# K and V of tile pairs by seven block products, earlier statistics, and one Q group moved among the output units

## The chip, the cores and the metric

The kernel runs on one core of a Trainium2 chip. The metric is the device time of one execution in microseconds. Before the change it is 757.27 us (median of three runs, 757.07 to 757.32). Engines are named as in the profile: PE is TensorE (matmuls, with PEld for its weight loads), DVE is VectorE, ACT is ScalarE, POOL is GpSimd, and SP is the engine that issues most of the DMAs. L428 is line 428 of the kernel before.

## The reference

Two blocks share a layer norm of x (2048 tokens, 1024 features): linear attention with 32 heads, and a SwiGLU feed-forward with 3584 hidden features. The output is x + s * silu(ffn). What the change touches is the projection of the normalized x to q, k and v, and the phi applied to q and k.

```python
def _layernorm(x, axis=-1, eps=1e-5):
    m = jnp.mean(x, axis=axis, keepdims=True)
    v = jnp.var(x, axis=axis, keepdims=True)
    return (x - m) / jnp.sqrt(v + eps)

def _A_ref(x, wqkv, wo):
    B, S, D = x.shape
    H = 32; Dh = D // H
    qkv = transpose((x @ wqkv).reshape(B, S, 3, H, Dh), 2, 0, 3, 1, 4)
    q, k, v = qkv[0], qkv[1], qkv[2]
    phi = lambda t: jnp.where(t > 0, t + 1, jnp.exp(t)) + 1e-6
    pq, pk = phi(q), phi(k)
    kv = jnp.einsum("bhsd,bhse->bhde", pk, v)
    z = jnp.einsum("bhsd->bhd", pk)
    num = jnp.einsum("bhqd,bhde->bhqe", pq, kv)
    den = jnp.einsum("bhqd,bhd->bhq", pq, z)[..., None] + 1e-6
    return transpose(num / den, 0, 2, 1, 3).reshape(B, S, D) @ wo

x = A_x
xn = _layernorm(x, axis=-1)
s = _A_ref(xn, A_wqkv, A_wo)
g = _silu((_silu(xn @ w_gate) * (xn @ w_up)) @ w_down)
return x + s * g
```

## The kernel before

**Stages.** The kernel is one long program of three stages. The front (L256 to L596) normalizes x, transposes it, and computes K, V and most of Q. The second stage (L598 to L724) finishes Q, computes the attention output tile by tile and multiplies it with wo. The third (from L728, about 500 us) is the feed-forward and the output. Tokens are cut into 16 tiles of 128, four blocks of four tiles (512 tokens), and two passes of two blocks (1024 tokens).

**Order.** In the front, `tc.manual_schedule` fixes the order of PE, DVE, ACT and POOL to the order in which the Python code emits instructions; SP's order is left to the scheduler. In the second stage SP's order is fixed too. Each engine works strictly through its own stream, so an instruction that waits holds up everything behind it on that engine. Work for DVE that has no place of its own stands in the deque `later`, and `fill(n)` emits the next n entries at fixed points.

**A tile in the front.** `emit_B(i, c)` is the c-th of four products of tile i with the K and V weights, 8 matmuls of 512 columns each (L428). The first two are K: ACT makes exp and relu of each (L186, L187), and after the second DVE makes phi from them (L190, L191). The last two are V, copied by ACT (L446). `emit_C(i)` adds the tile's 8 outer products of phi(k) and v (129 columns, L457) to the sums `kvz_ps`; it stands behind the first product of the next tile. For tiles 4 to 15 the loop at L568 emits the four products, two fillers behind each, and `emit_C` of the tile before.

**Statistics and transposes.** `emit_stats` (two instructions, L322) and `emit_aggr` (L335) give mean and variance of a tile; `emit_rstd` (L349) turns those of a group of tiles into 1/std with three DVE and twelve POOL instructions of a few columns; `emit_norm` (L371) applies them. Tiles 0 to 7 are transposed on PE (`emit_T`, the copies out of PSUM by DVE and then ACT). Blocks 2 and 3 (tiles 8 to 11 and 12 to 15) are written to DRAM and read back by a transposing DMA, both from SP (`emit_xT_block`, L415 and L416). In `later`, block 2's write is entry 18, behind the statistics of tiles 8 to 13.

**Q by block products.** `QGroup` computes 256 columns of q for one pass of 1024 tokens. The product is a 2 x 2 block product done with seven block products in place of eight (28 matmuls of 512 columns for 32). Part a: M3 into X, ACT copies X to u, M4 into Y, DVE adds Y to u. Part b: M1 into Z, DVE adds Z to u; M5 is added to X and M2 to Y, which then hold two of the four results, and ACT makes exp and relu of each. Part c: N7 is added to X and N6 to Y, DVE subtracts each from u, and ACT makes exp and relu of the two results. Part d is phi on DVE. The operands of the products are block sums made by DVE beforehand: `xsum_ops(p)` (five instructions of 2048 columns, L138) for x, `wsum_ops` (four, L152 to L155) for each group's weights. There are eight groups (pass 0 and 1, four each): six stand inside tiles 9 to 14, two, `qa` and `qb`, at the start of the second stage.

**PSUM.** All products of these stages draw from one pool of five buffers (`psB`); a buffer is free again behind its last reader.

**Second stage.** `emit_KVZ` masks the sums (DVE). `emit_ND(b, t)` is a tile's numerator and denominator (L632) with DVE's division behind it, and `emit_OT` writes the tile to DRAM (from ACT) and reads it back transposed (from SP, L656). An output unit `s_unit` is 8 matmuls with wo (L669), two for each tile; there are 32. The sets `nd_at` and `row_at` say before which unit an ND tile or a part d is emitted. Behind the last tile's `emit_OT` the first gate and up weights are loaded, and their block sums are made (`sum_w`) when four units are left.

**Memory that is used twice.** The eight tiles `xp`, each a pair of x tiles, lie in the pool `wgu` whose buffers later hold the q results `pqT`, and the normalized tiles wait for their transposition in `ws_all`, which later holds the block sums of weights.

Of the kernel before, what the change touches and what calls it, by code (L numbers as in the profile page):

```python
# [21 lines left out]
def kernel(  # L22
# [11 lines left out]
    nc = tc.nc  # L34
# [159 lines left out]
    wqp = p12.enter_context(tc.tile_pool(name="wqp", bufs=1))  # L194
    phiw = p12.enter_context(tc.tile_pool(name="phiw", bufs=5))
    qtmp = p12.enter_context(tc.tile_pool(name="qtmp", bufs=2))

    wq_sb = wqp.tile([P, DC, D], BF16, name="wq_sb")
    NM_Q = D // FW
    pqT_tiles = {}  # L200

    def exp_tile():
        return phiw.tile([P, SP_TOK], BF16, name="e_t", tag="e_t")

    class QGroup:


        def __init__(self, p, m):
            w = wq_sb[:, :, m * FW:(m + 1) * FW]
            self.lhs, self.rhs = block_operands(w, ws_all[:, m // 2, m % 2]), x_operands(p)  # L210
            self.out = wgu.tile([P, 2, SP_TOK], BF16, name="pqT", tag=("wg_sb" if m % 2 == 0 else "wu_sb"))
            pqT_tiles[(p, m)] = self.out
            self.row = {}
# [35 lines left out]
        def part_d(self, i):  # L249
            emit_phi(self.out[:, i, :], self.row[i][:])  # L250

    ET = mybir.EngineType
    FRONT_ORDER = {ET.PE, ET.DVE, ET.Activation, ET.Pool}
    kvz_ps = [psA.tile([P, GPT, NDW], FP32, name=f"kvz{j}", tag="A") for j in range(NJ)]
    with ExitStack() as p1:
# [4 lines left out]
        wkv_sb = wpool.tile([P, DC, 2 * D], BF16, name="wkv_sb")  # L260
        NV = 3
        v_bufs = [wpool.tile([P, G, NDW], BF16, name=f"v_sb{k}") for k in range(NV)]
# [85 lines left out]

        def emit_rstd(i):  # L349

            mv, rstd, tiles = grp_state[grp_of[i]]
            n = len(tiles)
            a = small.tile([P, TPB], FP32, name="lna", tag="lna")
            nc.vector.tensor_scalar(out=a[:, 0:n], in0=mv[:, 0:n, 1], scalar1=EPS_LN, scalar2=None, op0=ALU.add)
            yi = rstd[:, 0:n].bitcast(I32)
            nc.vector.tensor_single_scalar(out=yi, in_=a[:, 0:n].bitcast(I32), scalar=1, op=ALU.arith_shift_right)
            nc.vector.tensor_scalar(out=yi, in0=yi, scalar1=-1, scalar2=0x5f3759df, op0=ALU.mult, op1=ALU.add)
            y = rstd[:, 0:n]
            w = small.tile([P, TPB], FP32, name="lnw", tag="lnw")
            eng = nc.gpsimd  # L360
            for _ in range(NR_ITERS):
                eng.tensor_tensor(out=w[:, 0:n], in0=y, in1=y, op=ALU.mult)
                eng.tensor_tensor(out=w[:, 0:n], in0=w[:, 0:n], in1=a[:, 0:n], op=ALU.mult)
                eng.tensor_scalar(out=w[:, 0:n], in0=w[:, 0:n], scalar1=-0.5, scalar2=1.5,
                                  op0=ALU.mult, op1=ALU.add)
                eng.tensor_tensor(out=y, in0=y, in1=w[:, 0:n], op=ALU.mult)
# [15 lines left out]
        def xn_blk_slot(b):  # L382
            o = xn_base + (1 - b % 2) * TPB * D
            return ws_flat[:, o:o + TPB * D].rearrange("p (t d) -> p t d", t=TPB).bitcast(FP16)
# [35 lines left out]
        kv_tiles = {}  # L420

        def v_of(i):
            return v_bufs[i % NV]

# [24 lines left out]
        def emit_B(i, c):  # L449
            emit_B_mm(i, c)  # L450
            emit_B_out(i, c)

        def emit_C(i):
            pk_sb, v_sb = pk_tiles.pop(i), v_of(i)
            for g in range(G):
                j, gi = divmod(g, GPT)
                nc.tensor.matmul(kvz_ps[j][:, gi, 0:P + 1], lhsT=pk_sb[:, g * P:(g + 1) * P],  # L457
                                 rhs=v_sb[:, g, 0:P + 1],
                                 start=(i == 0 and gi == 0), stop=(i == NT - 1),
                                 skip_group_check=True)  # L460
# [10 lines left out]


        later = deque()
        for b in range(2, NB):
            for t in range(TPB):
                later.append(lambda i=b * TPB + t: emit_stats(i, parts=(0,)))
                later.append(lambda i=b * TPB + t: (emit_stats(i, parts=(1,)), emit_aggr(i)))
            later.append(lambda i=b * TPB: emit_rstd(i))
            if b > 2:
                for t in range(TPB):  # L480
                    later.append(lambda b=b, t=t: emit_norm(b * TPB + t, xn_blk_slot(b)[:, t, :]))
                later.append(lambda b=b: emit_xT_block(b))
            else:
                norm_b2 = [lambda b=b, t=t: emit_norm(b * TPB + t, xn_blk_slot(b)[:, t, :]) for t in range(TPB)]
                norm_b2.append(lambda b=b: emit_xT_block(b))

        pos = 2 * TPB + 1 + 4
        later = deque(list(later)[:pos] + norm_b2 + list(later)[pos:])
        later.extend(xsum_ops(0))
        for m in range(NM_Q):  # L490
            later.extend(wsum_ops(wq_sb[:, :, m * FW:(m + 1) * FW], ws_all[:, m // 2, m % 2]))
        later.extend(xsum_ops(1))

        def fill(n):
            for _ in range(min(n, len(later))):
                later.popleft()()

        with tc.manual_schedule(engines=FRONT_ORDER):
# [62 lines left out]
            emit_T(TPB + 1)  # L561
            emit_B_out(3, 2)
            emit_B(3, 3)
            fill(2)

            Q0 = 2 * TPB + 1
            early = deque([(0, m) for m in range(NM_Q)] + [(NPASS - 1, m) for m in range(NM_Q - 2)])
            for i in range(TPB, NT):  # L568
                grp = QGroup(*early.popleft()) if i >= Q0 and early else None
                nf = 1 if grp else 2  # L570
                emit_B(i, 0)
                fill(nf)
                emit_C(i - 1)
                if grp:
                    grp.part_a()
                emit_B(i, 1)
                fill(nf)
                if grp:
# [3 lines left out]
                emit_B(i, 2)  # L582
                fill(nf)
                if i == TPB:
# [4 lines left out]
                if grp:  # L589
                    grp.part_d(0)  # L590
                    grp.part_d(1)
                fill(nf)
            emit_C(NT - 1)
            assert not later and not early
        gate([x_loads[i] for i in range(first_wave, NT)], marks[("B", 1)], sync=True)
        gate(wq_loads, marks[("B", 3)], sync=True)  # L596

    with ExitStack() as p2:  # L598
# [90 lines left out]
        with tc.manual_schedule(engines=FRONT_ORDER | {ET.SP}):  # L689

            qa, qb = (QGroup(NPASS - 1, m) for m in (NM_Q - 2, NM_Q - 1))
            for c in range(NCC):
                nc.sync.dma_start(out=wo_sb[:, :, c * CW:(c + 1) * CW], in_=wo_v[:, :, c * CW:(c + 1) * CW])
            emit_KVZ()
            qa.part_a()
            qa.part_b()
# [10 lines left out]

            rows = deque((grp, i) for grp in (qa, qb) for i in range(2))
            nd_at = {1, 2, 4, 6, 8, 10, 11, 12, 14, 15, 16, 18, 19}
            row_at = {3, 5, 7, 9}  # L710
            assert len(nd_at) == len(nds) and len(row_at) == len(rows)
            u = 0
            while units:
                if u in nd_at:
                    nd_tile()
                if u in row_at:
                    grp, i = rows.popleft()
                    grp.part_d(i)
                if len(units) == 2 * NCC:
                    sum_w(0, 0)  # L720
                    sum_w(0, 1)
# [377 lines left out]
```

## Time and profile before

| What | Value |
|---|---|
| runs | 757.27 us median (757.07 to 757.32) |
| the profiled execution | 756.84 us, its span 755.1 us |
| granted TensorE clock | 1.000 throughout |
| front, second and third stage by PE | about 0 to 166, 166 to 242, 242 to 755 us |
| tile 8 begins | 70.0 us |
| last L457 of the front | 166.4 us |
| output units | 179.5 to 242 us |
| DVE busy, 60 to 80 us | 16.1 of 20 us |
| DVE and ACT busy, 77.4 to 165.9 us | 47.8 and 53.6 of 88.5 us |

The span runs from the first to the last instruction on the core; the execution's own time has 1.7 us more. Busy time of an engine counts each instruction's whole record. Matmuls overlap in these records, so how fast they follow each other is read from their starts and not from their lengths. In the lists of groups the columns are line, engine, operation, out<-in, shapes, count, then busy us and mean ns of one, then the idle time before and who ended it.

### The profile page before, as it was taken

What the parts mean: (1) busy time and instruction counts of PE and PEld (TensorE: products, weight loads), DVE (VectorE), ACT (ScalarE), POOL (GpSimd) and SP (SyncE); (2) the same over time, 40 slices, a digit from 0 to 9 for tenths busy, and PEclk for the clock granted to TensorE, in tenths of its full rate; (3) what the DMA queues carried; (4) which work ended last, traced back from release to release, by engine and by line L of the source; (5) the groups of instructions that cost most, each with busy time, mean ns of one, the idle gap of its engine ahead of it and who ended that gap; (6) DMA issues with size and microseconds to landing.
All of it is one profiled execution on the core that took longest, in us unless ns stands there. A gap on an engine that the chain in (4) does not pass through costs nothing.

```text
span 755.1 us, 9916 instructions
## 1 busy us (share of the span) xinstructions
PE 745.4 (99%) x3724; PEld 351.9 (47%) x3764; DVE 482.9 (64%) x897; ACT 276.3 (37%) x482; POOL 52.6 (7%) x112
## 2 busy tenths in 40 slices
PE   8999999999999999999999999999999999999997
PEld 3554444445554444444444444444444444444454
DVE  6686666348854677786787776876754754445453
ACT  4444556555223434333433434343343011111111
POOL 3311000000000000000000000000000222222220
PEclk9999999999999999999999999999999999999999
DMA  9606100017799534663355733544869845454300
GB/s 317 222 20 181 44 1 0 1 34 204 207 226 289 160 104 130 188 196 112 102 163 150 215 102 120 174 147 123 288 231 352 295 181 181 181 181 155 110 29 29
DMA packets 127663, 115.98 MB, mean 154 GB/s; under 512 B 29440, under 2 KB 108416, under 8 KB 126336
## 3 DMA queue, kind: packets, MB, share of 16 engines
q1 hardware_dynamic: 122720, 106.58, 45.8%
q10 hardware_dynamic: 4896, 8.78, 3.4%
q8 instruction: 29, 0.48, 0.3%
q14 instruction: 18, 0.15, 0.1%
HBM read 70.52 MB, written 38.54 MB: 144 GB/s over the span
## 4 chain that ended last, share of the span: by engine, by line
PE 95%; DVE 2%; DMA 1%; ACT 1%; issue 1%; DVEq 0%; ACTq 0%
PE X L131 29%; PE Y L131 28%; PE kv_ps L428 14%; PE Z L131 10%; PE s_ps L669 6%; PE qY L131 3%; PE qX L131 3%; PE kvz L457 1%; PE qZ L131 1%; PE nd_ps L632 1%; DVE stats L322 0%; DMA oT<-o_dram 0%; PE tr_ps L397 0%; DMA o_dram<-o_sb 0%; DMA xp<-in_A_x_dram 0%
## 5 line engine op out<-in xcount | busy, mean ns | idle before, releaser
L131 PEld LDWEIGHTS <-ws_all 128*128 128x128 bf16 x1420 | 137.8, 98 | 162.6 <-issue 0.2
L428 PE MATMUL kv_ps<-wkv_sb,xnT 128*128 128x512 bf16 x496 | 114.2, 379 | 1.2 <-DVE xnT L411 0.5
L762 DVE TENSOR_TENSOR q<-n,Y 128x512 f32<-128x512 f32 x63 | 43.4, 688 | 108.1 <-PE Y L131 104.9
L131 PEld LDWEIGHTS <-xs 128*128 128x128 bf16 x616 | 58.0, 98 | 63.1
L1032 POOL TENSOR_TENSOR o_out<-y,xres 128x512 bf16<-128x512 f32 x29 | 35.2, 1214 | 648.8 <-DVE y L1031 648.8
L428 PEld LDWEIGHTS <-xnT 128*128 128x128 f16 x512 | 49.2, 98 | 57.6 <-DVE xnT L411 0.7
L131 PE MATMUL Y<-xs,ws_all 128*128 128x512 f16 (+3 forms) x308 | 70.3, 360 | 0.0
L131 PE MATMUL X<-xnT,ws_all 128*128 128x512 f16 (+1 forms) x278 | 70.1, 379 | 0.2
L131 PE MATMUL Z<-xs,ws_all 128*128 128x512 f16 x224 | 57.5, 379 | 0.0
L131 PE MATMUL Y<-xnT,ws_all 128*128 128x512 f16 x224 | 57.5, 379 | 0.0
L131 PE MATMUL X<-xs,ws_all 128*128 128x512 f16 x224 | 57.5, 379 | 0.0
L886 ACT ACTIVATE g<-cg 128x512 bf16<-128x512 f32 x56 | 35.3, 631 | 54.1 <-DVE cg L777 54.1
L768 DVE TENSOR_TENSOR u<-Z,q 128x512 f32<-128x512 f32 x63 | 43.3, 687 | 16.0 <-PE Z L131 15.9
L886 ACT ACTIVATE g<-X 128x512 bf16<-128x512 f32 x28 | 16.7, 597 | 99.4 <-PE X L131 99.4
L758 ACT COPY n<-X 128x512 f32<-128x512 f32 x63 | 36.9, 586 | 27.1 <-PE X L131 26.7
L911 DVE TENSOR_TENSOR ho<-g,up 128x1024 bf16<-128x1024 bf16 x56 | 38.2, 686 | 0.5
L1031 DVE TENSOR_TENSOR y<-y,s_in 128x512 f32<-128x512 f32 x31 | 22.2, 717 | 21.8 <-ACT y L1025 15.8
L131 PEld LDWEIGHTS <-wu_sb 128*128 128x128 bf16 x224 | 21.9, 98 | 26.4
L131 PEld LDWEIGHTS <-wg_sb 128*128 128x128 bf16 x224 | 21.9, 98 | 26.4
L673 ACT CAST s_sb<-s_ps 128x512 bf16<-128x512 f32 x32 | 18.5, 586 | 42.1 <-PE s_ps L669 35.1
L1025 ACT ACTIVATE y<-X 128x512 f32<-128x512 f32 x8 | 4.8, 598 | 69.7 <-PE X L131 61.2
L186 ACT ACTIVATE e_t<-kv_ps 128x512 bf16<-128x512 f32 x32 | 19.2, 599 | 29.6 <-PE kv_ps L428 27.3
(140 smaller groups left out, 1044.2 us busy)
## 6 DMA issues: line engine op xcount, KB each, us to landing
h_dram<-ho SPq DMA_DIRECT2D x56, 256.0 KB, 2.5
wg_sb<-in_B_w_gate_dram SPq DMA_DIRECT2D x14, 512.0 KB, 4.0
wu_sb<-in_B_w_up_dram SPq DMA_DIRECT2D x14, 512.0 KB, 4.3
wdr<-in_B_w_down_dram SPq DMA_DIRECT2D x14, 512.0 KB, 4.2
ws_all<-h_dram SPq DMA_DIRECT2D x4, 1792.0 KB, 8.5
wds_dram<-wdsA SPq DMA_DIRECT2D x14, 384.0 KB, 2.6
hp_a<-h_dram SPq DMA_DIRECT2D x3, 1792.0 KB, 9.8
o_dram<-o_sb ACTq DMA_DIRECT2D x16, 256.0 KB, 3.1
```

The source lines that it names most:

```text
L131: marks["mm"] = nc.tensor.matmul(acc[:, 0:c1 - c0], lhsT=lhs(k), rhs=rhs(k)[:, c0:c1], start=(first and k == 0), stop=(k == n - 1), skip_g ...
L186: nc.scalar.activation(out=e, in_=t, func=ACT.Exp)
L428: mm = nc.tensor.matmul(kv_ps[:], lhsT=xn_tok_ap(i)[:, dc, :], rhs=wkv_sb[:, dc, c * CW:(c + 1) * CW], start=(dc == 0), stop=(dc == DC - 1))
L669: mm = nc.tensor.matmul(s_ps[:], lhsT=oT[:, c, ttok], rhs=wo_sb[:, c, cc * CW:(cc + 1) * CW], start=(c == 0), stop=(c == G - 1))
L673: nc.scalar.copy(out=s_sb[:, cc * CW:(cc + 1) * CW], in_=s_ps[:])
L758: nc.scalar.copy(out=n[:], in_=self.X[:])
L762: nc.vector.tensor_tensor(out=self.q[:], in0=n[:], in1=self.Y[:], op=ALU.add)
L768: nc.vector.tensor_tensor(out=self.u[:], in0=Z[:], in1=self.q[:], op=ALU.add)
L886: nc.scalar.activation(out=self.g[:, i, j * TB:(j + 1) * TB], in_=src, func=ACT.Silu)
L911: nc.vector.tensor_tensor(out=self.ho[:, i], in0=self.g[:, i], in1=self.up[:, i], op=ALU.mult)
L1031: nc.vector.tensor_tensor(out=t[:], in0=t[:], in1=self.s_in[:, i, cs], op=ALU.mult)
L1032: (nc.vector if last and (i, j) != (0, 0) else nc.gpsimd).tensor_tensor(out=self.o_out[:, i, cs], in0=t[:], in1=self.xres[:, i, cs], op=AL ...
```

## The change

The front's loop is taken apart. Tiles 4 to 8 and tile 12 are still computed one by one, in the order 4, 5, 6, 7, 8, 12. K and V of the pairs (10, 14) and (11, 15), and K of the pair (9, 13), are computed by a new class `KVGroup` with the same seven block products as `QGroup`; V of (9, 13) stays plain. The two tiles of a pair lie in blocks 2 and 3, so the block sums of x for pass 1 serve as left operands, and ten new DVE sums of the K and V weights (`kv_sum_ops`) as right ones. These sums are stored in two pqT tiles, in quarters of xnT that nothing reads any more, and in place in `wkv_sb`. The groups follow each other in a written sequence `seq`; part c and the phi (`post`) of a group are emitted behind part a of the next.

In `later`, statistics of all tiles 8 to 15 now come ahead of block 2's norms, the second `emit_rstd` runs all its twelve small instructions on DVE, and two empty entries are put in behind it. The write of block 2 is entry 25. The loop's fills are larger for tiles 4 to 7 (3, 2, 2, 2) and one `fill(2)` is added in front of the last product of tile 3.

Of the eight Q groups one stands in tile 12, four and the first part of a fifth (`qa`) in `seq`, `qa`'s rest and `qb` at the start of the second stage, and the eighth, `qc`, before output units 2, 3 and 4. `nd_at` and `row_at` are shifted to fit.

```diff
-    phiw = p12.enter_context(tc.tile_pool(name="phiw", bufs=5))
+    phiw = p12.enter_context(tc.tile_pool(name="phiw", bufs=4))
...
+    def alloc_pqT():
+
+        for p in range(NPASS):
+            for m in range(NM_Q):
+                pqT_tiles[(p, m)] = wgu.tile([P, 2, SP_TOK], BF16, name="pqT", tag=("wg_sb" if m % 2 == 0 else "wu_sb"))
...
-        NV = 3
+        NV = 4
...
-        def emit_rstd(i):
+        def emit_rstd(i, eng=nc.gpsimd):
...
-            eng = nc.gpsimd
...
-            o = xn_base + (1 - b % 2) * TPB * D
+            o = xn_base + b % 2 * TPB * D
...
+        def kv_sum_ops(which, places):
+            w = wkv_sb[:, :, which * D:(which + 1) * D]
+            w11, w12, w21, w22 = w[:, 0:HD, 0:CW], w[:, 0:HD, CW:D], w[:, HD:DC, 0:CW], w[:, HD:DC, CW:D]
+            s1, s5, s2 = places
+            kv_rhs[which] = {"M4": lambda k: w22[:, k, :], "M3": lambda k: w11[:, k, :], "M1": lambda k: s1[:, k, :],
+                             "M5": lambda k: s5[:, k, :], "M2": lambda k: s2[:, k, :],
+                             "N7": lambda k: w21[:, k, :], "N6": lambda k: w12[:, k, :]}
+            tt = nc.vector.tensor_tensor
+            return [lambda: tt(out=s1, in0=w11, in1=w22, op=ALU.add), lambda: tt(out=s5, in0=w11, in1=w21, op=ALU.add),
+                    lambda: tt(out=s2, in0=w12, in1=w22, op=ALU.add),
+                    lambda: tt(out=w21, in0=w22, in1=w21, op=ALU.subtract),
+                    lambda: tt(out=w12, in0=w11, in1=w12, op=ALU.subtract)]
...
+        class KVGroup:
+
+
+            def __init__(self, which, t):
+                self.which, self.rhs = which, kv_rhs[which]
+                xop = x_operands(NPASS - 1)
+                self.lhs = {n: (lambda k, f=f: f(k)[:, t * P:(t + 1) * P]) for n, f in xop.items()}
+                self.tiles = [(NB - 2 + j) * TPB + t for j in range(2)]
...
+            def direct(self, i, j, acc):
+                if self.which == 0:
+                    cs = slice(i * CW, (i + 1) * CW)
+                    emit_exp_relu(self.e[j][:, cs], self.pk[j][:, cs], acc[:])
+                else:
+                    nc.scalar.copy(out=self.v_out(i, j), in_=acc[:].rearrange("p (g c) -> p g c", c=P))
...
+            def part_c(self):
+                for acc, which, i in ((self.X, "N7", 0), (self.Y, "N6", 1)):
+                    self.mm(acc, which, False)
+                    if self.which == 0:
+                        cs = slice(i * CW, (i + 1) * CW)
+                        r = self.pk[i][:, cs]
+                        nc.vector.tensor_tensor(out=r, in0=self.u[:], in1=acc[:], op=ALU.subtract)
+                        emit_exp_relu(self.e[i][:, cs], r, r)
+                    else:
+                        nc.vector.tensor_tensor(out=self.v_out(i, i), in0=self.u[:].rearrange("p (g c) -> p g c", c=P),
+                                                in1=acc[:].rearrange("p (g c) -> p g c", c=P), op=ALU.subtract)
...
+        later.extend(stats_ops(NB - 2) + [lambda: emit_rstd((NB - 2) * TPB)] + stats_ops(NB - 1))
+        later.extend([lambda: emit_rstd((NB - 1) * TPB, nc.vector), None, None])
+        for ops in (norm_ops(NB - 2), norm_ops(NB - 1), xsum_ops(0), ws_ops(0)):
+            later.extend(ops)
+
+        def more_ops():
+
+            alloc_pqT()
+            k_ops = kv_sum_ops(0, (pq_place(NPASS - 1, NM_Q - 2), pq_place(NPASS - 1, NM_Q - 1), x_quarter(0, 0, 1)))
+            v_ops = kv_sum_ops(1, (x_quarter(0, 1, 0), x_quarter(1, 0, 1), x_quarter(1, 1, 0)))
+            for ops in (ws_ops(1), xsum_ops(NPASS - 1), k_ops, v_ops[:1], ws_ops(2), v_ops[1:], ws_ops(3)):
+                later.extend(ops)
...
+            rest = list(range(TPB, 2 * TPB)) + [b * TPB for b in range(2, NB)]
+            fills = {2 * TPB: (2, 2, 1, 1), rest[-1]: (2, 2, 1, 1)}
...
+            for i in rest:
+                nf = fills.get(i, (3, 2, 2, 2))
+                if i == 2 * TPB:
+                    more_ops()
+                grp = QGroup(0, 0) if i == rest[-1] else None
...
+            seq = [(lambda: Q(0, 1), 1, 1), (lambda: K(1), 0, 1), (VPlain, 2, 2), (lambda: Q(0, 2), 1, 1),
+                   (lambda: K(2), 1, 1), (lambda: V(2), 2, 2), (lambda: Q(0, 3), 0, 0), (lambda: K(3), 0, 0),
+                   (lambda: Q(NPASS - 1, 0), 0, 0), (lambda: V(3), 0, 0), (lambda: Q(NPASS - 1, 1), 0, 0)]
+            prev = None
+            for make, fa, fb in seq:
+                grp = make()
+                grp.part_a()
+                fill(fa)
+                if prev:
+                    prev.part_c()
+                    prev.post()
+                else:
+                    emit_C(before)
+                if make is not seq[-1][0]:
+                    grp.part_b()
+                    fill(fb)
+                while ready_C:
+                    emit_C(ready_C.popleft(), last=(not ready_C and make is seq[-1][0]))
+                prev = grp
+            qa = prev
...
-            qa, qb = (QGroup(NPASS - 1, m) for m in (NM_Q - 2, NM_Q - 1))
+            qb, qc = QGroup(NPASS - 1, NM_Q - 2), QGroup(NPASS - 1, NM_Q - 1)
...
-            qa.part_a()
...
-            nd_at = {1, 2, 4, 6, 8, 10, 11, 12, 14, 15, 16, 18, 19}
-            row_at = {3, 5, 7, 9}
+            nd_at = {1, 2, 4, 6, 8, 11, 12, 13, 15, 16, 17, 19, 20}
+            row_at = {2, 3, 5, 7, 9, 10}
+            q_at = {2: qc.part_a, 3: qc.part_b, 4: qc.part_c}
...
+                if u in q_at:
+                    q_at[u]()
```

`KVGroup`'s parts a and b are those of `QGroup`, with its own names for the PSUM tiles (kX, kY, kZ) and with `direct` for the two results that part b completes: for K exp and relu by ACT, for V one copy by ACT.

## The prediction

> **What bounds the kernel now.** I read the page first, then TensorE's waits, then the timelines of TensorE, VectorE and the SP queue over the stretch that the change rebuilds (39 to 190 us), then the rows by shape.
>
> ```profile
> span 755.1 us, 9916 instructions
> ...
> PE 745.4 (99%) x3724; PEld 351.9 (47%) x3764; DVE 482.9 (64%) x897; ACT 276.3 (37%) x482; POOL 52.6 (7%) x112
> ```
>
> ```profile
> PE w_ps L466 <- DVE warm L90: 1.2, 1, 1.2
> PE s_ps L669 <- DMA oT<-o_dram: 0.5, 2, 0.3
> PE kv_ps L428 <- DVE xnT L411: 0.5, 1, 0.5
> ```
>
> ```profile
> 49.86 0.39 PE L457 MATMUL kvz<-v_sb,pk_sb 128*128 128x129 bf16 x4 [0.20 <-ACT v_sb L446]
> ...
> 72.19 7.07 PE L428 MATMUL kv_ps<-wkv_sb,xnT 128*128 128x512 bf16 x32
> 79.09 0.62 PE L457 MATMUL kvz<-v_sb,pk_sb 128*128 128x129 bf16 x8
> ```
>
> A busy share of 99% proves little, since a matmul's record (379 ns) outlasts its slot. What shows the bound is starts: 32 matmuls take 72.19 to 79.09, 0.216 us each, and TensorE's whole list of waits is about 3 us. From 50 to 179 us I find no other hole (holes of exactly one slot every ten us or so are missing records). So TensorE's own instruction stream sets the end, a removed 512-column matmul is worth 0.216 us, and a new wait of TensorE is paid in full.
>
> **What is removed.** A K or V product of two tiles was 2 x 2 x 8 = 32 matmuls; by block products it is 7 x 4 = 28. Five groups use it (K of 9/13, 10/14, 11/15; V of the last two): 20 matmuls, 20 x 0.216 = 4.32 us. The 129-column matmuls (L457) and all eight Q groups stay; one Q group of 28 x 0.216 = 6.05 us moves from the front to the output units. So 4.32 is all that the removal can give.
>
> The stream of weight load and matmul has been priced lower elsewhere: the Trainium skill (TensorE: Matmul & The Clock Gate, section Back-to-back issue gap) says a 512-column matmul in such a stream costs about 131 ns, by which 20 would give 2.6 us and my sum would end 1.7 us higher. This trace disagrees with its 216 ns, and the measurement decides.
>
> **What is added, by engine.** Rows by shape (after the bar: busy us, mean ns of one, then idle time before):
>
> ```profile
> L138 DVE TENSOR_TENSOR xs<-xnT 128x2048 f16<-128x2048 f16 x10 | 11.8, 1218 | 0.0
> L191 DVE TENSOR_TENSOR pqT<-e_t,pqT 128x1024 bf16<-128x1024 bf16 x16 | 11.1, 692 | 2.3 <-ACT pqT L187 1.9
> L231 DVE TENSOR_TENSOR qu<-qu,qY 128x512 f32<-128x512 f32 x8 | 5.5, 687 | 10.2 <-PE qY L131 10.2
> L228 ACT COPY qu<-qX 128x512 f32<-128x512 f32 x8 | 4.7, 586 | 2.5 <-PE qX L131 2.3
> L186 ACT ACTIVATE e_t<-pqT 128x512 bf16<-128x512 bf16 x16 | 9.9, 621 | 9.6 <-DVE pqT L246 9.6
> ```
>
> VectorE: ten weight sums of 2048 elements at 1.22 = 12.2 us, and four combinations of 0.69 in each of five groups = 13.7 us. ScalarE: one copy of 0.59 a group, less two copies in each V group. From the start of tile 8 to the last L457 TensorE then has tile 8 (7.4), tile 12 with a Q group (13.4), nine groups of 28 matmuls, the plain V of 9/13 with 32, eight of the last Q group's first part (292 x 0.216 = 63.1) and seven L457 batches of 0.46: 87.1 us. VectorE has 72 us in it: phi of tiles 8 and 12 (2.2), K groups 3 x (4 x 0.69 + 2 x 1.11) = 14.9, V groups 5.5, Q groups 25.6, sums 24.1 (weights of Q 5.8, block sums of x 6.1, the ten new ones 12.2). It fits in total, but each engine works in order, so lateness in single steps counts. I walked the steps with these durations.
>
> At nothing I take three edits. Four exp tiles for five: never more than four are live, and the oldest is given back by phi a whole step (6 us) before its next writer; a phi that late would stop ScalarE. The pqT tiles handed out at tile 8 need the last norm of tile 15, done near 63 us, while their first writer comes near 86. The sums' places in xnT and pqT were last read at least 5 us before (V's second and third sum follow the plain V products by 3 us).
>
> *Tiles 4 to 7.* Statistics of all eight tiles now come first; the write of block 2 moves from place 18 of the filler list to 25. Up to it VectorE has, from 39.51 us: eight tiles' statistics at 1.43 = 11.44, the first rstd 0.47, two phi at 1.14, two transposed copies at 0.29, four norms 1.92, and the second rstd, now on VectorE: 3 + 12 dependent instructions of four columns. VectorE shows only the first three, 0.16 long and 0.205 apart; between 0.16 (no gap) and GpSimd's 0.28 pitch I take 0.2, so 2.9 (2.3 to 3.9). With 0.6 idle at phi of tile 5 this ends at 59.6 instead of 56.5. Two costs:
>
> ```profile
> 56.52 0.39 SPq L415 DMA_DIRECT2D xn_dram<-ws_all  x1
> 61.27 3.99 SPq L416 DMA_TRANSPOSE xnT<-xn_dram  x1
> 68.63 0.39 SPq L415 DMA_DIRECT2D xn_dram<-ws_all  x1
> 72.94 4.04 SPq L416 DMA_TRANSPOSE xnT<-xn_dram  x1
> ```
>
> Write to landing is 4.75 us, then a transpose of 6.05 (10.8). Block 2 lands at 59.6 + 10.8 = 70.4; tile 8 wants it at 70.0. And block 3 is wanted by tile 12, now directly behind tile 8, at 77.4, no longer at about 118. Its norms are done by 63.3, but on SP its write stands behind block 2's transpose, which waits for its own write until 64.4 and then holds SP for 4.0: issue at 68.4, landing at 78.8 to 78.9. TensorE waits until then: **+1.5** in all, the 0.4 of tile 8 and 0.2 more at L457 (its ScalarE copy stands behind the later transposed copy) included. Should SP send block 3's write first, it lands in time and delays block 2's transpose instead, at most by its own three microseconds of data: +0.4 to +3.0. No case lies below nothing, since an earlier landing frees nothing that TensorE waits for today. GpSimd loses its twelve instructions (63.36 to 66.65 today), for which VectorE stood 3.4 us.
>
> *Groups.* Per step ScalarE has 5.4 us (a copy and eight activations) against 6.05 of TensorE where a K or Q group follows a K or Q group, plus 1.5 in which it must wait for VectorE's two combinations. Two such steps in a row stay inside the slack that N7 and N6 leave (0.7 and 0.6 us); V groups give it back. Where VectorE puts sums ahead of a subtraction the chain slips: K(2) holds V's two in-place sums, V(2) the sums of the last Q weights. By my walk K(2)'s N7 and N6 wait 0.25, V(2)'s N7 0.7 (its M5 copy stands behind K(2)'s four activations), C(12) 0.1: **+1.05** (0 to 3).
>
> *Last group.* L457 of 11 and 15 follows V(3)'s last products with nothing between: 0.16 drain + 0.69 subtraction against 0.86 of N6, then again for N6: **+0.35** (0, if later products go ahead of it, to 1.1).
>
> *Output units.* The moved Q group stands before units 2, 3 and 4, exactly where TensorE waits today:
>
> ```profile
> 184.34 3.63 PE L669 MATMUL s_ps<-wo_sb,oT 128*128 128x512 bf16 x16 [0.19 <-DMA oT<-o_dram]
> 188.78 3.40 PE L669 MATMUL s_ps<-wo_sb,oT 128*128 128x512 bf16 x15 [0.34 <-DMA oT<-o_dram]
> ```
>
> With the 0.16 by which a record outlasts its slot, 0.35 and 0.50 go: **-0.85** (-0.85 to +0.5: VectorE has 12.5 us of work in these 14.4). The first unit's cover shrinks by nothing: from Q part b to it the order is unchanged; the KVZ masks (2.0 us of VectorE) lose the first part but fit under part b's 2.6. The loads of the first gate weights are triggered one unit later (1.7 us); today they land at 234.7 and 236.2 and TensorE reaches their product at 242.5, so that hides.
>
> **Sum.** -4.32 + 1.5 + 1.05 + 0.35 - 0.85 = -2.3: span 755.1 to 752.8. The profiled execution took 756.84, 1.7 beyond its span, the median of the runs is 757.27: 755.0.
>
> **Rivals.**
> *No new waits* (chance 0.20): blocks 2 and 3 land in time, or ScalarE and VectorE stay ahead; -4.3 - 0.85 plus at most 1.5: 752.1 to 753.6. For it: ScalarE is busy 53.6 of 88.5 us from 77.37 to 165.9 today. Against: VectorE was busy 7.24 of 7.37 us in tile 7 already, and the SP rows leave block 3 no room.
> *Transposes collide* (0.14): write of 3 and transpose of 2 share the DMA queues, which either fills alone (about 380 and 290 GB/s), and the twelve small instructions take GpSimd's pitch: +3 to +4 in place of 1.5, so 756.5 to 757.5, no change.
> *ScalarE becomes the bound of the groups* (0.18), the slower side: each of the seven steps behind a K or Q group takes 5.4 + 1.5 = 6.95 instead of 6.05, 7 x 0.9 = 6.3; -4.32 + 1.5 + 6.3 + 0.35 - 0.85 = +3.0: 760.2. It decides from the point where ScalarE ends the activation of Y more than 2.6 us after M2, when N6 must wait. Against: steps behind V need only 3.0 us of ScalarE. What would start it is a PSUM buffer handed out late, but today kv_ps starts at 129.29 while VectorE's subtraction from X still runs (128.62 to 129.31), so X's buffer is not the next one used.
> *The forecast* (0.48): 753.9 to 756.4 around 755.0.
>
> About 0.2%, 1.5 us, can be told from no change. Faster by that: most of the forecast (0.42) and the first rival, 0.62; within it 0.06 and 0.12 of the collision, 0.18; slower 0.20. The range leaves out the slow case and the lowest tip: 752.5 to 758.0.
>
> **What the profile would show.** 512-column block products on kX, kY, kZ: 140, and 160 fewer L428. First matmul of tile 12 waiting for the transpose, released near 79 us, the block 3 write near 68.4. VectorE within 3 us of its work in the group steps, waits of TensorE on ScalarE at N7 or N6 of V(2). The two waits for oT before units 2 and 4 gone. I am wrong if TensorE has many waits of about 0.9 us from 100 to 160, or none at tile 12.

## The result, and the profile after

| | before | after |
|---|---|---|
| runs, median | 757.26 us (22 runs, 756.41 to 758.39) | 759.57 us (22 runs, 756.99 to 762.48) |
| ratio of after to before | | 1.0031 (95% interval 1.0021 to 1.0041) |
| the profiled execution | 756.84 us, span 755.1 | 760.91 us, span 759.1 |
| mean granted clock of the profiled execution | 1.000 | 0.996 |

The change made the kernel 0.31% slower; forecast was 0.3% faster, and the time lies outside the range. The removed work is gone all the same (3704 records of matmuls in place of 3724). Three far slower executions, one of e3 (870 us), one of e7 (2816 us) and one of the kernel before beside e5 to e8 (2833 us), enter no median and no ratio below. The page of the kernel after, and TensorE's waits (cause, us in total, times, longest):

```profile
span 759.1 us, 9917 instructions
...
PE 743.6 (98%) x3704; PEld 350.8 (46%) x3744; DVE 507.5 (67%) x939; ACT 275.9 (36%) x483; POOL 50.1 (7%) x101
```

```profile
PE s_ps L822 <- DMA oT<-o_dram: 3.0, 1, 3.0
PE kv_ps L440 <- DMA xnT<-xn_dram: 2.8, 1, 2.8
...
PE kv_ps L440 <- DVE xnT L419: 0.5, 1, 0.5
PE kvz L469 <- ACT v_sb L458: 0.5, 1, 0.5
PE kX L131 <- ACT v_sb L531: 0.4, 1, 0.4
```

Before, the longest wait for a transfer was 0.3 us. Now there are two of 3 us: at the first product of tile 8 (L440) and before output unit 0 (L822). The timeline of TensorE around tile 8, and the windows before and behind it (length, then busy us and instructions of PE, PEld, DVE, ACT and POOL, granted clock, DMA share, GB/s):

```profile
65.33 5.34 PE L440 MATMUL kv_ps<-wkv_sb,xnT 128*128 128x512 bf16 x24
73.50 2.72 PE L440 MATMUL kv_ps<-wkv_sb,xnT 128*128 128x512 bf16 x7 [2.82 <-DMA xnT<-xn_dram]
76.44 1.07 PE L469 MATMUL kvz<-v_sb,pk_sb 128*128 128x129 bf16 x8 [0.22 <-issue]
77.30 6.91 PE L440 MATMUL kv_ps<-wkv_sb,xnT 128*128 128x512 bf16 x31
```

```profile
70.00:74.00 4.00, 1.18 (x7) 0.37 (x5) 2.92 (x7) 0.58 (x1) 0.00 (x0) 1.00 1.13 232
74.00:77.40 3.40, 3.18 (x15) 1.74 (x15) 0.00 (x0) 0.66 (x2) 0.00 (x0) 0.50 0.91 205
```

The third number from the end is the clock: 1.00 during the wait, then 0.50 for 3.4 us, though TensorE is working again. The eight L469 take 0.86 us from the first to the next product there, 0.46 elsewhere. So one wait costs twice: 2.99 us until the data come, then 3.41 x 0.5 = 1.7 us of work at half clock. A profile whose clock stayed at 1.000 there (e3, below) agrees: from tile 8's first product to the first one behind the wait of V(2) it takes 60.11 us, the kernel after 61.78.

The sum of the prediction beside what the starts in this trace give (us beyond the usual pitch of each product):

| Step | Forecast | Measured |
|---|---|---|
| 20 products removed | -4.32 | -4.32 |
| L457 of tile 4 (later transposed copy) | +0.2 | +0.30 |
| tile 8 waits for block 2 | +0.4 | +2.99 |
| half clock behind it | not in the sum | +1.7 |
| tile 12 waits for block 3 | about +1 | 0 |
| K(2), V(2), C(12) | +0.25, +0.7, +0.1 | +0.29, +0.53, 0 |
| last group | +0.35 | +0.08 |
| unit 0 waits for oT | 0 | +3.15 |
| waits before units 2 and 4 | -0.85 | -0.85 |
| span | -2.3 | +3.9 (755.1 to 759.1 is +4.0) |

Three rows make the error: tile 8, the clock and unit 0 are 7.4 us over the forecast, and the rows of tile 12 and the groups give back some 1.3. Over the runs of this kernel the clock shows again: of the 22 times, the 14 with a mean granted clock of 0.997 or less lie at 758.82 to 762.48, the 8 above that at 756.99 to 759.57. (Up to 0.002 of the mean is half clock behind the last matmul, which costs nothing. Of 76 runs of the kernel before, taken beside e1 to e10, one has 0.997 and none less.)

### The profile page after: what moved, and what is told of

Its sections match the earlier page's. It is cut to its first block, busy times and chain, and to the rows that moved or that the text cites. A ratio compares the mean times of both kernels' runs of the same rounds, so it can differ in the third digit from the quotient of the medians.

```text
span 759.1 us, 9917 instructions
## 1 busy us (share of the span) xinstructions
PE 743.6 (98%) x3704; PEld 350.8 (46%) x3744; DVE 507.5 (67%) x939; ACT 275.9 (36%) x483; POOL 50.1 (7%) x101
## 4 chain that ended last, share of the span: by engine, by line
PE 91%; DVE 4%; DMA 3%; ACT 1%; issue 1%; DVEq 0%; ACTq 0%
PE X L131 29%; PE Y L131 28%; PE Z L131 10%; PE s_ps L822 7%; PE kv_ps L440 6%; PE qY L131 2%; PE qX L131 2%; PE kY L131 1%; PE kX L131 1%; DMA xnT<-xn_dram 1%; PE nd_ps L785 1%; PE kvz L469 1%; DVE stats L331 1%; DMA o_dram<-o_sb 1%; PE qZ L131 1%
## 5 line engine op out<-in xcount | busy, mean ns | idle before, releaser
L131 PEld LDWEIGHTS <-xs 128*128 128x128 bf16 (+1 forms) x716 | 67.6, 98 | 75.3 <-issue 1.2
L440 PE MATMUL kv_ps<-wkv_sb,xnT 128*128 128x512 bf16 x342 | 79.8, 383 | 3.8 <-DMA xnT<-xn_dram 2.8
L440 PEld LDWEIGHTS <-xnT 128*128 128x128 f16 x352 | 33.9, 99 | 42.7 <-DMA xnT<-xn_dram 3.3
L822 PE MATMUL s_ps<-wo_sb,oT 128*128 128x512 bf16 x123 | 29.0, 379 | 3.2 <-DMA oT<-o_dram 3.0
```

What stands on the lines that cost most here:

```text
L131: marks["mm"] = nc.tensor.matmul(acc[:, 0:c1 - c0], lhsT=lhs(k), rhs=rhs(k)[:, c0:c1], start=(first and k == 0), stop=(k == n - 1), skip_g ...
L440: mm = nc.tensor.matmul(kv_ps[:], lhsT=xn_tok_ap(i)[:, dc, :], rhs=wkv_sb[:, dc, c * CW:(c + 1) * CW], start=(dc == 0), stop=(dc == DC - 1))
L822: mm = nc.tensor.matmul(s_ps[:], lhsT=oT[:, c, ttok], rhs=wo_sb[:, c, cc * CW:(cc + 1) * CW], start=(c == 0), stop=(c == G - 1))
```

## Experiments

All are edits of the kernel after. The ratio is to the kernel before on the same chip; for the kernel after itself it is 1.0031. The waits (us beyond pitch) and the span are those of the one profiled execution.

| Run | median | ratio (95%) | span, clock | tile 8 | tile 12 | units 0 to 2 |
|---|---|---|---|---|---|---|
| e1_order | 757.78 | 1.0007 (0.9998 to 1.0016) | 755.2, 0.999 | 0.20 | 1.31 | 2.33 |
| e2_rstd_pool | 756.14 | 0.9987 (0.9978 to 0.9995) | 755.8, 0.996 | 0 | 0.28 | 3.01 |
| e3_qc_early | 759.30 | 1.0018 (1.0007 to 1.0028) | 755.3, 1.000 | 2.70 | 0 | 1.31 |
| e4_busy | 757.62 | 0.9999 (0.9990 to 1.0007) | 755.6, 0.999 | filled | 0 | 1.36 |
| e5_pool_qc | 755.37 | 0.9974 (0.9965 to 0.9983) | 753.2, 1.000 | 0 | 0.19 | 1.31 |
| e6_wo_half | 759.64 | 1.0033 (1.0014 to 1.0052) | 757.4, 0.996 | 2.84 | 0 | 2.39 |
| e7_pool_half | 756.15 | 0.9985 (0.9974 to 0.9997) | 754.0, 0.999 | 0 | 0.53 | 2.20 |
| e8_plain | 759.67 | 1.0031 (1.0019 to 1.0043) | 757.9, 1.000 | 0 | 0.64 | 2.21 |
| e9_wo_split | 756.12 | 0.9980 (0.9971 to 0.9989) | 755.0, 0.999 | 0.09 | 1.37 | 2.12 |
| e10_wo_only | 759.46 | 1.0028 (1.0019 to 1.0038) | 758.3, 0.996 | 2.76 | 0 | 2.78 |
| e11_cover | 754.86 | 0.9963 (0.9951 to 0.9975) | 753.1, 1.000 | 0 | 1.05 | 0.62 |

**The order on SP (e1_order).** The issue records of SP in the kernel after: block 2's write 60.07, block 3's write 63.59, block 2's transpose 64.45 to 70.53, block 3's transpose 70.63. The scheduler, which chose SP's order, put block 3's write ahead of block 2's transpose; the prediction had it behind. The edit holds it behind:

```diff
-            nc.sync.dma_start(out=blk_rows_pt(xn_dram, b), in_=xn_blk_slot(b))
-            nc.sync.dma_start_transpose(out=xn_blk_ap(b), in_=blk_rows(xn_dram, b))
+            wr = nc.sync.dma_start(out=blk_rows_pt(xn_dram, b), in_=xn_blk_slot(b))
+            gate([wr], marks.get("xT"))
+            marks["xT"] = nc.sync.dma_start_transpose(out=xn_blk_ap(b), in_=blk_rows(xn_dram, b))
```

> The changed kernel with one scheduling edge: block 3's write is issued on SP behind block 2's transpose. Theory (the write overtook on SP and shares the DMA engines with the transpose, which then lands at 73.45 us): block 2 lands at 60.1 + 10.8 = 70.9 and tile 8 waits 0.5 us in place of 3.0; block 3 is issued near 68.5, lands near 79, and tile 12 now waits about 1.0. No wait is long, so the granted clock stays 1.000 and the 1.7 us at half clock go: span 759.1 - 2.5 - 1.7 + 1.0 = 755.9. Rival (VectorE's lateness alone makes block 2 late, the order on SP is nothing): the transpose still takes 9 us from issue to landing, tile 8 waits 3.0 and the time stays near 759.6.

The queue of SP in e1 (start, length, line, transfer):

```profile
60.00 0.39 SPq L423 DMA_DIRECT2D xn_dram<-ws_all  x1
64.38 4.13 SPq L425 DMA_TRANSPOSE xnT<-xn_dram  x1
68.61 0.53 SPq L423 DMA_DIRECT2D xn_dram<-ws_all  x1
73.26 3.99 SPq L425 DMA_TRANSPOSE xnT<-xn_dram  x1
```

and in the kernel after, where the trace joins the pairs:

```profile
60.07 3.91 SPq L423 DMA_DIRECT2D xn_dram<-ws_all  x2
64.45 10.66 SPq L424 DMA_TRANSPOSE xnT<-xn_dram  x2
```

The write begins at the same time in both. Alone, block 2's transpose holds SP 4.13 us and lands 6.21 us after its start (70.59); beside block 3's write it holds SP 6.08 us and lands after 9.00 (73.45). That is the 3 us of tile 8. With the edit tile 8 waits 0.20, tile 12 waits 1.31, which are the prediction's numbers for its own order (0.4 and about 1). No half clock follows, and the kernel is 0.24% faster than the kernel after. Four of its 12 runs still have a clock of 0.997; the wait before unit 0 is left in it.

**The twelve small instructions (e2_rstd_pool).**

```diff
-        later.extend([lambda: emit_rstd((NB - 1) * TPB, nc.vector), None, None])
+        later.extend([lambda: emit_rstd((NB - 1) * TPB), None, None])
```

> The changed kernel with the second 1/std back on GpSimd, one argument less. Theory (collision on the DMA engines, set off because block 2's norms come 2.4 us later on VectorE): block 2's write goes at 57.7, its transpose at 62.4, ahead of block 3's write (63.6 or later), so it lands at 68.5 and tile 8 waits for nothing; block 3 lands by 77, in time for tile 12; clock 1.000. 759.1 - 3.0 - 1.7 = 754.4 span. Rival (the same collision at another time): block 3's write still stands ahead of the transpose, tile 8 waits 1 us or more. Rival (1/std on GpSimd holds VectorE up as it did before): block 3's norms wait 3 us and tile 12 waits 2 to 3.

Block 2's write starts at 57.58 in place of 60.07, and the scheduler's order on SP is that of e1 (transpose at 63.30, second write at 67.43). Both blocks land in time but for 0.28 us at tile 12, and the median falls 0.44%. The edit changes two things at once, the 2.5 us and the order; e1 shows the order alone. The span is 755.8 us where 754.4 was expected, and the clock of 0.996 in this profile comes from elsewhere than tile 8: it was 0.5 from 172.79 to 176.20, around the end of the 3.01 us wait before unit 0 (which starts at 173.53).

**The clock by itself (e4_busy).** Twelve matmuls of zeros into an unused PSUM tile stand where TensorE waits; nothing arrives sooner.

```diff
+                    d_ps = psB.tile([P, TB], FP32, name="d_ps", tag="B")
+                    for _ in range(12):
+                        nc.tensor.matmul(d_ps[:], lhsT=warm[:, 0:P], rhs=warm[:], start=True, stop=True)
```

> The changed kernel with twelve matmuls of zeros put in front of tile 8, 2.6 us of TensorE work that is in nobody's way while it waits 3.0 us for block 2. Theory (the wait itself lets the granted clock fall to one half for 3.4 us, in some executions and to different parts, and that makes the times spread from 757.0 to 762.5): clock 1.000 in all runs, the wait of tile 8's first real matmul the same, 757.2 in nearly all runs. Rival (the spread has another source, the DMAs for one): the runs still reach from 757 to 762.

Its timeline at tile 8 and the same two windows:

```profile
70.85 2.75 PE L686 MATMUL d_ps<-warm 128*128 128x512 bf16 x11
73.44 1.89 PE L440 MATMUL kv_ps<-wkv_sb,xnT 128*128 128x512 bf16 x8
75.17 0.62 PE L469 MATMUL kvz<-v_sb,pk_sb 128*128 128x129 bf16 x8
```

```profile
70.00:74.00 4.00, 3.95 (x19) 1.82 (x19) 3.26 (x7) 0.59 (x1) 0.00 (x0) 1.00 1.09 239
74.00:77.40 3.40, 3.40 (x24) 1.77 (x22) 0.00 (x0) 1.08 (x2) 0.00 (x0) 1.00 1.09 226
```

Tile 8 begins as late as in the kernel after, at 73.44 for 73.50, but at full clock, and none of the 11 runs has a clock under 0.998; they lie at 756.52 to 758.28, so the rival, another source of the spread, is out. The median is 0.32%, some 2.4 us, under the kernel after for more work done. The profiled half-clock stretch is worth 1.7 of it; how the other 0.7 splits between it and unit 0's wait, here 1.36 us and not 3.15, the runs do not tell.

**The wait before unit 0.** The engine queues of the kernel after (SP, then ACT, then TensorE):

```profile
163.62 1.80 SPq L846 DMA_DIRECT2D wo_sb<-in_A_wo_dram  x2
174.56 16.44 SPq L809 DMA_TRANSPOSE oT<-o_dram  x5
```

```profile
168.37 0.35 ACTq L808 DMA_DIRECT2D o_dram<-o_sb  x1
```

```profile
174.13 1.02 PE L131 MATMUL qY<-xs,ws_all 128*128 128x512 f16 x4
178.14 1.90 PE L822 MATMUL s_ps<-wo_sb,oT 128*128 128x512 bf16 x7 [2.99 <-DMA oT<-o_dram]
```

wo's 2 MB are issued behind the last L469 of the front and land at 170.17 and 173.39. The first tile's write (o_dram), issued at 168.37, lands at 174.54, 6.17 us later, and its transpose at 178.10. From wo's issue to oT there are 14.5 us; TensorE has 11.4 us of work in them (to 174.99). Before the change the chain was 166.58 to 179.02, 12.4 us (wo landed at 172.01 and 175.28, the write at 175.64), and TensorE had 12.9 us of work, to 179.46, because `qa`'s part a (1.73 us) stood there too. This edit puts matmuls there again, the moved Q group before units 0 and 1:

```diff
-            rows = deque((grp, i) for grp in (qa, qb, qc) for i in range(2))
+            rows = deque((grp, i) for grp in (qb, qc) for i in range(2))
...
-            row_at = {2, 3, 5, 7, 9, 10}
-            q_at = {2: qc.part_a, 3: qc.part_b, 4: qc.part_c}
+            row_at = {5, 7, 9, 10}
+            q_at = {0: lambda: (qc.part_a(), qa.part_d(0), qa.part_d(1), qc.part_b()), 1: qc.part_c}
```

> The changed kernel with the moved Q group's parts a and b before output unit 0 and part c before unit 1 (the phi of the first group goes ahead of part b). Theory (unit 0 waits for a chain of DMAs that starts when wo's load is issued behind the last L469, with the first o write behind wo's 2 MB): the transposed o lands about 14.5 us after that issue whatever TensorE does, so 4.3 us more of matmuls cover it, the 3.15 us wait goes, and the waits before units 2 and 4 do not come back: -3.1. Rival (the division on VectorE is late): the wait stays at 2 us or more, now with VectorE named ahead of it. The tile 8 wait and the half clock stay in both, so the times spread as in the changed kernel, around 756.4.

The wait for oT is gone. In its place part b's second product waits 1.31 us for the ScalarE copy of X, which follows part a too closely. The tile 8 wait stays. The profiled execution, which has no half-clock stretch, took 757.10 us, but the median is 759.30 where 756.4 was expected: by the ratios 0.13% below the kernel after, and the two intervals overlap. Four of the 9 runs have a clock of 0.996 or 0.997. Together with e2's edit:

> The twelve small instructions are back on GpSimd (as in e2) and the last Q group's parts stand before units 0 and 1 (as in e3). Theory (the kernel loses time only by TensorE's two 3 us waits and by the half-clock stretches that such a wait can start; the two waits are independent): no wait at tile 8, as in e2; the wait before unit 0 falls from about 3 to about 1.3 us, as in e3, too short for a half-clock stretch, so the clock is 1.000 in most runs: 1.5 to 2.5 us below e2, 753.6 to 754.6. Rival (the spread of e3's runs has another cause than tile 8's wait, for example the Q group's own place): clock 0.996 to 0.998 in most runs as in e3, 755.5 to 757.5.

The ratio is 0.9974, and no clock of the 9 runs is under 0.998: what was left of e3's time was tile 8's. Beside e2 (0.9987) that is 1.0 us, where 1.5 to 2.5 were expected, and the intervals overlap.

Does the write wait for wo? The second half of wo (read first by unit 1) is issued behind the first transpose, on the kernel after (e6) and with e2's edit (e7):

```diff
-            for c in range(NCC):
+            def load_wo(c):
                 nc.sync.dma_start(out=wo_sb[:, :, c * CW:(c + 1) * CW], in_=wo_v[:, :, c * CW:(c + 1) * CW])
+            load_wo(0)
...
             emit_OT()
+            load_wo(1)
             qa.part_c()
```

> Only the order of SP is changed against the kernel after: the second half of wo (columns 512 to 1023, read first by unit 1) is issued behind the transpose of the first ND tile, no longer in front of it. Theory (the first ND tile's write, issued about 4.5 us behind the loads of wo, queues behind their 2 MB and takes 6 us where 2 would do): the write lands within 2.5 us of its issue, the transpose about 2.5 us later, and TensorE reaches unit 0 with a wait of at most 0.5 us; the tile 8 wait and its half-clock stretch stay: 2 to 3 us below the kernel after, 756.5 to 757.5. Rival (the write is slow by itself, or the transpose is): the wait before unit 0 stays at 1.3 to 3 us and unit 1 waits for the second half as well: 759.5 to 762.

> e6's order of wo together with e2's GpSimd instructions: neither of the two 3 us waits should be left. Theory: clock 1.000 in most runs, TensorE's waits only about 0.3 at tile 12, 0.3 in K(2), 0.5 in V(2): span 755.1 - 4.32 + 0.3 (C of tile 4) + 0.3 + 0.3 + 0.5 - 0.85 = 751.3, time 753.1 (752.5 to 753.8), about 0.5% below the kernel before. Rival (each wait removed comes back elsewhere, at tile 12 or before units 1 and 2): 755 to 756.5, no better than e2.

SP's queue and TensorE's first wait in e7:

```profile
159.11 0.39 SPq L846 DMA_DIRECT2D wo_sb<-in_A_wo_dram  x1
166.26 1.24 SPq L809 DMA_TRANSPOSE oT<-o_dram  x1
167.55 0.57 SPq L846 DMA_DIRECT2D wo_sb<-in_A_wo_dram  x1
174.76 2.59 SPq L809 DMA_TRANSPOSE oT<-o_dram  x2
```

```profile
PE s_ps L822 <- DMA wo_sb<-in_A_wo_dram: 1.6, 1, 1.6
```

The mechanism held and the remedy failed. The write took 2.76 us in e6 and 2.38 in e7, for 6.17, and e7's oT landed at 169.37, 3.5 us ahead of TensorE. But unit 0 then waited until wo's second half landed (174.43), and no time was won: the rival's times. Unit 0 does not read that half; both halves lie in one tile, and with a tile for each (below) the wait at unit 0 is gone.

So e9 gives each half a tile, issues the second behind two transposes, and exchanges units 1 and 2 so that it is read later; e10 is the same without e2's edit.

```diff
-        wo_sb = wop.tile([P, G, D], BF16, name="wo_sb")
+        wo_h = [wop.tile([P, G, CW], BF16, name=f"wo_sb{c}") for c in range(NCC)]
...
+        units[1], units[2] = units[2], units[1]
...
             qb.part_b()
             emit_OT()
+            load_wo(1)
             nd_tile()
```

> e2 with wo in two tiles of its own (columns 0 to 511 and 512 to 1023), the second one's load issued behind the transposes of the first two ND tiles, and output units 1 and 2 exchanged, so that the second half is read two units later. Theory (in e6 and e7 the write and transpose of the first ND tile were on time, landed at 169.4 in e7 against TensorE's 172.8, and unit 0 waited only for the other half of the one wo tile): unit 0 waits at most 0.3 us, units 1 to 3 at most 0.5 together, clock 1.000 in most runs: 2.5 to 3 us below the profile of e2, span 752.0 to 753.0, median 753.7 to 755.0. Rival (the 2 MB of wo, 1 MB of transposes and writes fill the queues anyway, and what is late only changes its name): waits of 1.5 us or more before units 1 to 3, median 755.3 to 756.5 as e5 and e7.

> The kernel after with e9's order of wo and units alone; the twelve small instructions stay on VectorE. Theory (the wait before unit 0 and the one at tile 8 are independent, and unit 0's costs about 2.7 us more than before the change): the tile 8 wait of 3 us and its half-clock stretch stay, unit 0's goes: 2 to 3 us below the kernel after, 756.5 to 757.6, no change against the kernel before; the difference to e9 is 2.5 to 3.5 us. Rival (the wait before unit 0 is a follow-up of the tile 8 stall): unit 0 waits as in e9, but e9 and this are within 1 us.

Unit 0 starts with no wait in e9, 172.07, but units 1 and 2 wait 1.07 (oT of the second tile, 175.28) and 1.05 (wo, 180.26). e10 has 1.27 and 1.51 there. The expected 2 to 3 us did not come; the lateness changed its name, as the rival said. What did hold is the difference of the two, 0.9980 to 1.0028, 3.6 us (3.3 by the medians) against 2.5 to 3.5 expected: tile 8's wait with its half clock, independent of unit 0. It agrees with e2 against after (0.44%, 3.3 us).

What helps is again matmuls that need neither transfer. e11 is e9 with the last Q group's parts one to two units earlier:

```diff
-            row_at = {2, 3, 5, 7, 9, 10}
-            q_at = {2: qc.part_a, 3: qc.part_b, 4: qc.part_c}
+            row_at = {1, 2, 5, 7, 9, 10}
+            q_at = {0: qc.part_a, 2: qc.part_b, 3: qc.part_c}
```

> e9 with the last Q group's part a before unit 0 (the cover of 1.73 us that the change took away there), part b before unit 2 and part c before unit 3; qa's two phi one unit earlier. Theory (units 1 and 2 of e9 waited 1.07 and 1.05 us only because the second ND tile's transpose and the second half of wo land at 175.3 and 180.3, and matmuls that need neither can stand there): unit 1 is reached 1.7 us later and unit 2 after part b's 2.6 us, so no wait over 0.3 us before units 0 to 3: 1.5 to 2 us below e9's span but for the transposes' own scatter, span 752.0 to 753.5, median 753.8 to 755.2. Rival (what lands late moves with TensorE, since the ND tiles' writes stand behind TensorE's own products): waits of 1 us or more stay before units 1 to 3, median 755.5 to 756.5.

```profile
PE kv_ps L440 <- DMA xnT<-xn_dram: 0.9, 1, 0.9
PE kv_ps L440 <- DVE xnT L419: 0.5, 1, 0.5
PE kvz L469 <- ACT v_sb L458: 0.5, 1, 0.5
PE kX L131 <- ACT v_sb L531: 0.4, 1, 0.4
```

These are TensorE's waits in e11 but for the one of 1.2 us at the very start, which the kernel before has too. No unit waits any more for oT or wo (0.62 us go in an L785 batch at 177.4). The median, 754.86 us, is 0.37% under the kernel before and 0.68% under the kernel after, and the six runs spread over 1.2 us.

**What the removal is worth (e8_plain).** e7 with the five K and V groups computed plainly: 20 matmuls more, no sums, no combinations.

```diff
+            class Plain:
...
+                def part_a(self):
+                    emit_B(self.tiles[0], self.which * NCC)
...
+                def part_b(self):
+                    for j, c in ((0, 1), (1, 0), (1, 1)):
+                        emit_B(self.tiles[j], self.which * NCC + c)
...
+            K, V = (lambda t: Plain(0, t)), (lambda t: Plain(1, t))
```

> e7 with the five K and V groups computed plainly again in the same sequence (32 matmuls instead of 28 each, no weight sums, no combinations on VectorE), everything else as in e7. Theory (a removed 512-column matmul is worth 0.216 us, and the groups' own waits cost 0.8): 20 x 0.216 = 4.3, less 0.8 of waits that go with the groups, so 3.5 us above e7 (3.0 to 4.2). Rival (VectorE's and ScalarE's added work in the groups gives most of the saving back): at most 2 us above e7.

e8's median is 3.5 us above e7's, and its waits at K(2), V(2) and the last group are gone. The rival's 2 us at most is out: VectorE's 26.7 us more work in e7 from 60 to 165 us (83.84 against 57.12) are nearly all hidden.

## Why the prediction was wrong

**Right.** The price of a removed product (0.216 us) and the count: putting the 20 products back costs e8 3.5 us, and 4.32 less the 0.9 us of the groups' own waits is 3.4. The groups: 0.82 us measured for 1.05, in two of the three places named (nothing at C(12)); V(2)'s wait ended with the ScalarE copy behind K(2)'s four activations, as walked. The twelve instructions: 0.20 us apart in the trace, and the write at 60.07 for 59.6. The waits before units 2 and 4 went. ScalarE did not become the bound: no row of waits from 100 to 160 us but those of K(2) and V(2), so the rival at 760.2 had the time and not the mechanism.

**The step that failed first** is "but on SP its write stands behind block 2's transpose". SP's order in the front is the scheduler's, as the text before the prediction says, and it chose otherwise. The fallback in the same paragraph, "+0.4 to +3.0", has the right mechanism, and the 2.99 is its upper end; the sum went by the other order, and the two orders' waits cannot be averaged. The rival on colliding transposes named the same mechanism; the front alone (0.30 + 2.99) came out in its +3 to +4, without GpSimd's pitch.

**The step that was missing** is the granted clock. The prediction read it as 1.000 throughout and took a wait as worth its own length ("a new wait of TensorE is paid in full"). In the profile the wait of tile 8 cost 1.7 us more, and 14 of the 22 runs have a clock of 0.997 or less; with matmuls in that wait (e4) none of 11 has.

**The step that failed last** is "The first unit's cover shrinks by nothing" (its cover is the work that TensorE has while the transfers for it are under way). The order from part b on is indeed the same, but the cover has to be counted from the event that starts the late chain, and that is wo's issue behind the last L469. Part a of `qa` stood behind that event and now stands in front of it; the work behind the event fell from 12.9 to 11.4 us. Against the old chain of 12.4 that would have left a wait of 1.0; the other 2.1 is the chain itself, 14.5 us: wo's second half lands 9.77 us after the issue of the first in place of 8.70, the write lands 1.15 us behind it in place of 0.36, though it now follows wo's issue by 4.75 us in place of 6.26, and the rest takes 0.2 us more. That size is not fixed: the same code showed 1.36 to 3.15 us in four profiles (after, e1, e2, e4).

With the three taken away the sum is the forecast: e11, which has the change's groups, SP's order as forecast and cover before the late units, spans 753.1 us, and 755.1 - 2.3 is 752.8. Its single terms agree less closely: with the twelve instructions on GpSimd tile 8 does not wait at all, and 0.62 us among the units stands in place of that 0.4.

What stays open: why the scheduler chose SP's two orders, why wo takes 8.38 us in one profile (e4) and 9.77 in another (after), with the chain before unit 0 as long behind it, and in how many runs of the kernel after the wait there starts a half-clock stretch too. It did in e2's profile and not in that of after.

## What to carry to other kernels

When work is moved, count the cover of the next late transfer from the event that releases the transfer's chain, not from the work in front of its reader, and ask for each queue whether its order is written down or chosen. Price a wait of TensorE of about 3 us at up to 1.7 us above its length, paid in some runs and not in others, and fill it with other matmuls first: moving products in front of a late reader gave more here (e11) than trying to make the transfer earlier (e6, e10). A transfer that looks like the cause may only be the last of several; e6, e9 and e10 each freed one and met the next.

## What the runs showed of the hardware

**Half clock after a wait.** Waits of TensorE of 2.76 (e10), 2.84 (e6), 2.99 (after) and 3.01 us (e2) were each followed by one stretch of 3.41 us at clock 0.5, which began between 0.7 us before and 0.5 us after TensorE went on. Waits of 2.70 (e3, tile 8) and 3.15 us (after, unit 0) were not, nor any of 2.4 us or less. The Trainium skill (TensorE: Matmul & The Clock Gate, section What's actually happening) has the array at half rate after at least one idle window of about 3.4 us, in windows that run freely. That the stretch lasts 3.41 us and comes in some runs only agrees with this; that a wait of 2.8 us is enough does not, by its letter, and the measurement decides.

The records of the clock show what decides in place of the wait's length. In the 13 profiles every stretch of one clock, up to the last change, is a whole number of windows of 3.413 us (1, 20, 49, 169, 199, 219 or 220), so the same windows can be laid over TensorE's busy time. Every whole window in which TensorE was busy for 1.39 us or less was followed by half clock: 0.59 in after (70.59 to 74.00), 0.81 in e10 (70.03 to 73.44), 1.30 in e2 (169.38 to 172.79), 1.39 in e6 (68.97 to 72.38), and those at the ends of the spans. Every one with 1.46 us or more kept the full clock: 1.46 at the end of e11 (746.81 to 750.22), 1.64 in e3 (68.90 to 72.31), and 2.17 and 1.61 in after (172.99 to 176.40 to 179.81), which divide the 3.15 us before unit 0 between them. So a wait counts by how much of one window it leaves empty. How it falls on the windows differs between executions: the first record of the clock lies 4.05 us into the span in e3 and 6.60 in e8.

**A write behind a load lands with the load.** A tile's 256 KB write from ACT, issued while wo's load from SP was under way, mostly landed just behind the load, however long that was: issued 168.37, landed 174.54 (wo 173.39) in after; 168.41, 174.74 (174.43) in e7; 174.81, 180.95 (180.26) in e9; 177.42, 184.21 (183.53) in e10. The first tile's write does the same in before, e1, e3 and e4, 0.4 to 1.0 us behind wo. One row differs: in e6 the second tile's write, issued 0.46 us behind wo's second half, landed 1.5 us ahead of it. The Trainium skill (DMA: Bandwidth & Descriptors, section Queues, rings and completion order) says that a DMA's completion on one DMA engine follows every earlier write of that engine, across its queues. The four rows fit this, and would fit mere sharing of the engines too; e6's row shows that the order of issue alone does not decide.

**A transpose beside a write.** The block transpose of 1 MB took 6.2 us alone and 9.0 with 1 MB being written beside it, and held its issuing queue for 6.1 us in place of 4.1.
